# A transform-and-expert kernel: second product three rounds behind the first, a new calendar, working buffers 32 bytes later

## The chip, the cores and the metric

One core of a Trainium2 chip runs the program. The metric is device time in microseconds (us), the median of several executions; a lower time is better. The kernel before takes 2706.86 us (three runs, 2706.52 to 2708.56).

## What is computed

Two stages follow each other on 8 sequences of 3008 tokens of 256 numbers each, in float32. Cut to what matters:

```python
X  = rfft(x, axis=1)                       # along the 3008 tokens
Yr = X.real @ w_r - X.imag @ w_i + b_r
Yi = X.real @ w_i + X.imag @ w_r + b_i
Y  = soft_threshold(Yr, 0.01) + 1j * soft_threshold(Yi, 0.01)
y  = irfft(Y, n=3008, axis=1)              # 24064 tokens of 256
h  = maximum(y @ w_in, 0)                  # 256 -> 2048
out = (h * h) @ w_out                      # 2048 -> 256
```

## The kernel before

Products are made in float32 accuracy from a high and a low part of each operand (float32r): a high part is a copy on ACT, the low part a subtraction on DVE, and `mm3` (L182 to L184) issues three matmuls for one product.

**Start.** `start()` transforms the first two sequences partly, loads and splits the weights, and makes the first chunk of transformed tokens. It ends 144.9 us into the span. The change touches it only in the addresses of its buffers.

**Main loop.** The tokens are cut in 47 chunks of 512 columns, the 2048 hidden features in 8 groups; 47 x 8 = 376 rounds. A round r of the main loop (L904 to L932) does, in this order of issue:

- `mm1` (PE, L182 to L184): the first product of round r, 12 matmuls of 512 columns into the PSUM tile `ph`, of which there is one (two banks).
- `squares` (ACT, L863 and L864): two Relu from `ph` into `g`, then a square in place. As soon as the Relu are done, `ph` is free for the next `mm1`.
- places "p1" (PE) and "e" (ACT): pieces of the transform that stand in the calendar for this round.
- the high part `gh` of the round before (ACT, L916).
- `mm2` (PE, L878 and L882): the second product, `LAG` = 2 rounds behind, 21 matmuls of 256 columns into the four banks of `po`, 14 with `gh` and 7 with `gl`. Over the 8 rounds of a chunk it adds up in these banks.
- `sums` (DVE, L869 to L871) on `g`, and the low part `gl` of the round before (DVE, L927).
- place "p2" (PE), then, in the last round of a chunk, `put_together` (ACT L889, DVE L890 to L896): it reads the four banks of `po`, and the output is stored. The next chunk's first `mm2`, one round later, writes the same banks.
- places "a" (ACT) and "v" (DVE).

**Transform pieces.** For the sequences 2 to 7 there are pieces of three kinds. An A piece (`plan_a`, `psa`, 6 matmuls of 256 columns) is evacuated by ACT (L679). A pair (`plan_b`) has `psb` (8 matmul records, evacuated by ACT, L223), two rounds on the mix `psm1`, `psm2` (18 matmuls of 256 columns, evacuated by DVE, L233 and L234), and later `psc` (3 matmuls of 512 columns, evacuated by ACT, L754). A D piece (`plan_d`, `psd`, 8 records) is evacuated by ACT (L784) and by the two `unfold` instructions of DVE (L275, L276). All of them share two PSUM banks, `ps_f`, in turn; the mix takes both. The other six banks are `ph` and `po`.

**Calendar.** `pair_rounds` fixes the rounds of the pairs; `spread` places the A and D pieces by a planner's cost, which adds up the work of the engines in each round and keeps A and D pieces out of the rounds of a mix. All pieces but the mix stand at "p1", between `mm1` and `mm2`, and up to three of them in one round. What is given to the places "a" and "v" is issued last in its round: the unfold of a D piece stands behind `gl` on DVE.

Of the kernel before, what the change touches and what calls it, by code (L numbers as in the profile page):

```python
# [9 lines left out]
F32 = mybir.dt.float32  # L10
F32R = mybir.dt.float32r
# [4 lines left out]
P = 128  # L16
# [4 lines left out]
NPAIR = NR // 2  # L21
# [117 lines left out]

def pair_rounds(nb):  # L140

    out = {1: [1, 3, 5, 7, 9, 11, 13, 15, 17, 19, 22, 25]}
    for b in range(2, nb):
        last = 25 + 48 * (b - 1)
        out[b] = [last - (3 if b == 2 else 4) * (NPAIR - 1 - i) for i in range(NPAIR)]
    return out


# [1 line left out]
def fft_mix_moe(ctx: ExitStack, tc: tile.TileContext, xp, xu, w_r, w_i, b_r, b_i,  # L150
# [75 lines left out]
    def sum_x(x):  # L226
        nc.vector.tensor_add(x[:, 2], x[:, 0], x[:, 1])
# [380 lines left out]
    kept = []  # L608
    start()

    sb = ctx.enter_context(tc.tile_pool(name="sb", bufs=1))
    ps_f = ctx.enter_context(tc.tile_pool(name="ps_f", bufs=2, space=bass.MemoryType.PSUM))
    ps_h = ctx.enter_context(tc.tile_pool(name="ps_h", bufs=1, space=bass.MemoryType.PSUM))
# [8 lines left out]
    def opnd(name, dt, bufs):  # L622
        return tl(name, (P, NPR, HALF), dt, bufs=bufs)

    rounds = pair_rounds(B)
    last = nch * NU
    plan = {}
    works = np.zeros((last + 64, 3))

    def at(r, place, do):  # L630
        plan.setdefault((r, place), []).append(do)
# [5 lines left out]
    def note(r, *steps):  # L637
        for d, *w in steps:
            works[r + d] += w

    PAIR_WORK = ((0, .9, .6, .4), (1, 0, .8, 1.), (2, 2.1, 0, 1.4), (3, 0, 0, 1.1), (4, 0, 1.8, 0),
                 (5, 0, .6, .7), (7, .7, .6, 0))
    A_WORK = ((-3, 0, 0, .8), (-2, 0, .6, .7), (0, .7, .6, 0))
    D_WORK = ((0, .9, .4, .8), (1, 0, .7, .7))
    SUM_WORK = (0, 0, .3, 2.9)

    def plan_a(b, i, r):
        g, w = GROUPS[i]
        n, tab = NR * w, 0 if w == W else 2
        s = {}  # L650

        def load():
            if i == 0:
                scratch1(b)
            s["t"] = tl("ld", bufs=2, name="xin")[:n]
            load_x(b, i, s["t"])

        def folded():
            s["f"] = tl("f", name="f")[:n]
            fold(s["f"], s["t"])  # L660

        def high():
            s["h"] = tl("fh", dt=F32R)[:n]
            nc.scalar.copy(s["h"], s["f"])

        def low():
            s["l"] = tl("fl", dt=F32R)[:n]
            nc.vector.tensor_sub(s["l"], s["f"], s["h"].bitcast(F32))

        def points():  # L670
            s["o"] = pst("psa")[:n]
# [12 lines left out]
        at(r - 2, "a", high)  # L684
        at(r - 2, "v", low)
        at(r, "p1", points)
        at(r, "e", out)

    def plan_b(b, i, r):
        s = {}  # L690
# [66 lines left out]
        at(r - 1, "load", load)  # L757
        at(r, "p1", points)
        at(r, "e", take)
        at(r, "v", lambda: sum_x(s["x"]))  # L760
        at(r + 1, "a", high)
        at(r + 1, "v", low)
        at(r + 2, "p2", mix)
        at(r + 2, "v", biased)
        at(r + 3, "v", threshold)
        at(r + 4, "a", turned)
        at(r + 5, "a", zhigh)
        at(r + 5, "v", zlow)
        at(r + 7, "p1", back)
        at(r + 7, "e", out)  # L770

    def plan_d(i, r, later):
        s = {}

        def load():
            s["t"] = tl("din")
            load_d(i, s["t"])

        def points():
            s["ps"] = points_d(i, s["t"], pst("psd"))  # L780

        def take():
            s["v"] = const.tile([P, 2 * NR * W], F32, tag="dv", name="dv").rearrange("p (k m) -> p k m", k=2)
            nc.scalar.copy(s["v"][:, :, :s["ps"].shape[3]], s["ps"][:, :, 1])  # L784

        def unfolded():
            s["x"] = const.tile([P, 2 * N1 * W], F32, tag="dx", name="dx").rearrange("p (k m) -> p k m", k=2)
            unfold(i, s["ps"], s["v"], s["x"])

        at(r - 1, "load", load)  # L790
        at(r, "p1", points)
        at(r, "e", take)
        at(r, "v", unfolded)
        for n, piece in enumerate(pieces(i)):
            q = later if n else r + 1
            at(q, "a", lambda piece=piece: high_x(piece, s["x"]))
            at(q, "v", lambda piece=piece: low_x(piece, s["x"]))

    for b, rs in rounds.items():
        for r in rs:  # L800
            note(r, *PAIR_WORK)
    for c in range(nch):
        works[c * NU + NU + 1] += SUM_WORK[1:]

    mixes = {r + 2 for rs in rounds.values() for r in rs}
    def spread(n, lo, hi, work, apart):

        best = [{} for _ in range(n)]
        for i in range(n):
            for r in range(lo, hi + 1):  # L810
                if r in mixes:
                    continue
                cost = sum(max(0., float(np.sum(works[r + d] + w))) ** 2 - float(np.sum(works[r + d])) ** 2
                           for d, *w in work)
                before = min(((c, q) for q, (c, _) in best[i - 1].items() if q <= r - apart),
                             default=None) if i else (0., ())
                if before is not None:
                    best[i][r] = before[0] + cost, (best[i - 1][before[1]][1] if i else ()) + (r,)
        got = min(best[-1].values())[1]
        for r in got:  # L820
            note(r, *work)
        return got

    begin = 3
    for b in range(2, B):
        end = rounds[b][0] - 3
        got = spread(len(GROUPS), begin, end, A_WORK, 2)
        begin = max(got[-1] + 2, rounds[b][0] - 12)
        for i, r in enumerate(got):
            plan_a(b, i, r)  # L830
# [6 lines left out]
    free = 2  # L837
    for c in range(1, nch):
        own = [i for i in range(len(flat)) if begins[i] // CH == c]
        parts = [[i for i in own if flat[i][0] == b] for b in sorted({flat[i][0] for i in own})]  # L840
        for n, part in enumerate(parts):
            b = flat[part[0]][0]
            lo = max(NU * (c - 1), free, rounds[b][-1] + 9 if b else 2)
            got = spread(len(part), lo, NU * c - 3 - sum(map(len, parts[n + 1:])), D_WORK, 1)
            free = got[-1] + 1
            for i, r in zip(part, got):
                plan_d(i, r, NU * c)

    def mm1(c, j):
        ph = ps_h.tile([P, 2, CH], F32, tag="h", name="ph")  # L850
# [48 lines left out]
                              in_=o[k].rearrange("p t m -> p (t m)"))  # L899

    hid, split_, pos = {}, {}, {}
    LAG = 2
    with tc.manual_schedule():
        for r in range(last + LAG):  # L904
            c, j = divmod(r, NU)
            run(r, "load")
            if r < last:
                ph = mm1(c, j)
                g = squares(ph)
                hid[r] = g  # L910
            run(r, "p1")
            run(r, "e")
            k = r - 1
            if k in hid:
                split_[k] = opnd("gh", F32R, 2), opnd("gl", F32R, 2)
                nc.scalar.copy(split_[k][0], hid[k])  # L916
            k = r - LAG
            if k >= 0:
                cc, jj = divmod(k, NU)
                if jj == 0:  # L920
                    pos[cc] = [ps_o.tile([P, 512], F32, tag=f"o{i}", name=f"po{i}") for i in range(4)]
                mm2(jj, pos[cc], *split_.pop(k))
            if r < last:
                sums(g)
            if r - 1 in hid:
                gh, gl = split_[r - 1]
                nc.vector.tensor_sub(gl, hid.pop(r - 1), gh.bitcast(F32))  # L927
            run(r, "p2")
            if k >= 0 and jj == NU - 1:
                put_together(cc, pos.pop(cc))  # L930
            run(r, "a")
            run(r, "v")  # L932
    assert not plan, sorted(plan)
# [38 lines left out]
```

## Time and profile before

| what | value |
|---|---|
| median of three runs | 2706.86 us |
| profiled execution, its own time | 2706.33 us |
| its span | 2704.2 us |
| PE busy | 2580.7 us (95%) |
| PE weight loads busy | 2288.4 us (85%) |
| DVE busy | 2112.6 us (78%) |
| ACT busy | 1982.9 us (73%) |
| chain that ended last | PE 72%, ACT 11%, DVE 7%, issue 7% |

The span is what the trace covers; 2.1 us of the profiled execution lie around it. PE is the engine with the most work. A matmul's record lasts longer than the time after which the next one starts, so the busy time of PE covers a part of the time in which it waits.

### The profile page before, as it was taken

Reading aid. Unit: us, or ns where it says so; the run is one execution under the profiler, and the core shown is the slowest. Engines: PE = TensorE matmul, PEld = TensorE weight load, DVE = VectorE, ACT = ScalarE, POOL = GpSimd, SP = SyncE. Lnnn points to the kernel's source line nnn. Section 1 sums busy time; section 2 is a strip of 40 time slices with the busy share of each in tenths; the row PEclk is TensorE's granted clock in tenths of the full one; section 3 lists DMA queues with packets and bytes.
Section 4 is the critical chain, followed back from the end, with each engine's and each line's share of the span. In section 5 each row is a group of like instructions: output and inputs, shape, how many; then the busy total and the mean of one; then the engine's idle time right before and its main releaser. Section 6 shows DMA issues by size and latency. Waiting matters only on the chain.

```text
span 2704.2 us, 41768 instructions
## 1 busy us (share of the span) xinstructions
PE 2580.7 (95%) x16496; PEld 2288.4 (85%) x16496; DVE 2112.6 (78%) x3155; ACT 1982.9 (73%) x2764; POOL 48.2 (2%) x57
## 2 busy tenths in 40 slices
PE   7889999999999999999999999999999999999998
PEld 4578888888888889888888888888888998888887
DVE  5777887877788878877888788887887778777776
ACT  4667776767777777777787777877777777776766
POOL 1500000000000000000000000000000000000000
PEclk8999999999999999999999999999999999999999
DMA  8522222211112111121112111211111111001000
GB/s 261 182 67 65 65 65 69 65 50 60 56 57 69 57 57 56 60 65 46 56 60 68 54 57 53 75 53 51 57 56 48 38 39 51 31 24 35 16 27 16
DMA packets 113092, 164.57 MB, mean 61 GB/s; under 512 B 9584, under 2 KB 63074, under 8 KB 112706
## 3 DMA queue, kind: packets, MB, share of 16 engines
q1 hardware_dynamic: 112898, 161.91, 19.3%
q8 instruction: 131, 2.15, 0.3%
q14 instruction: 63, 0.52, 0.1%
HBM read 86.90 MB, written 74.97 MB: 60 GB/s over the span
## 4 chain that ended last, share of the span: by engine, by line
PE 72%; ACT 11%; DVE 7%; issue 7%; DMA 1%; SPq 0%; DVEq 0%; ACTq 0%
PE po L878 17%; PE ph L184 10%; PE ph L182 10%; PE ph L183 10%; PE po L882 9%; ACT gh L916 4%; ACT g L863 4%; PE psd L268 3%; PE psm L184 2%; PE psm L182 2%; PE psm L183 2%; PE psb L219 1%; DVE gl L927 1%; PE psc L182 1%; ACT x L223 1%
## 5 line engine op out<-in xcount | busy, mean ns | idle before, releaser
L927 DVE TENSOR_TENSOR gl<-g,gh 128x1792 fp32r<-128x1792 f32 x376 | 761.2, 2025 | 144.2 <-ACT gh L916 144.1
L863 ACT ACTIVATE g<-ph 128x512 f32<-128x512 f32 x752 | 408.4, 595 | 592.0 <-PE ph L184 590.9
L878 PE MATMUL po<-gh,wo 128*128 128x256 f32 x5264 | 703.6, 284 | 29.2 <-DVE o L891 17.9
L878 PEld LDWEIGHTS po<-gh,wo 128*128 128x128 f32 x5264 | 657.9, 189 | 57.5 <-DVE o L895 16.7
L916 ACT CAST gh<-g 128x1792 fp32r<-128x1792 f32 x376 | 636.2, 1692 | 0.2 <-DVE g L871 0.2
L182 PE MATMUL ph<-xt,wi 128*128 128x512 f32 x1504 | 592.7, 394 | 10.1 <-DVE dx L276 8.8
L184 PE MATMUL ph<-xt,wi 128*128 128x512 f32 x1504 | 591.1, 393 | 0.0
L183 PE MATMUL ph<-xt,wi 128*128 128x512 f32 x1504 | 590.7, 393 | 0.0
L869 DVE TENSOR_TENSOR g<-g 128x512 f32<-128x512 f32 x376 | 259.9, 691 | 332.7 <-ACT g L864 331.6
L864 ACT ACTIVATE g<-g 128x1024 f32<-128x1024 f32 x376 | 398.9, 1061 | 11.9
L882 PE MATMUL po<-gl,wo 128*128 128x256 f32 x2632 | 369.1, 280 | 0.2 <-DVE gl L927 0.2
L184 PEld LDWEIGHTS ph<-xt,wi 128*128 128x128 f32 x1504 | 283.3, 188 | 64.6
L882 PEld LDWEIGHTS po<-gl,wo 128*128 128x128 f32 x2632 | 334.9, 188 | 0.4 <-DVE gl L927 0.4
L182 PEld LDWEIGHTS ph<-xt,wi 128*128 128x128 f32 x1504 | 283.5, 188 | 59.0 <-ACT xt L280 9.0
L183 PEld LDWEIGHTS ph<-xt,wi 128*128 128x128 f32 x1504 | 283.2, 188 | 47.9
L871 DVE TENSOR_TENSOR g<-g 128x256 f32<-128x256 f32 x376 | 159.9, 425 | 12.9
L870 DVE TENSOR_TENSOR g<-g 128x256 f32<-128x256 f32 x376 | 160.0, 425 | 12.8
L184 PE MATMUL psm<-wm,xl 128*128 128x256 f32 (+1 forms) x552 | 162.3, 294 | 0.7 <-DVE xl L712 0.6
L182 PE MATMUL psm<-wm,xh 128*128 128x256 f32 (+1 forms) x552 | 162.1, 294 | 0.3 <-ACT x L223 0.3
L183 PE MATMUL psm<-wm,xh 128*128 128x256 f32 (+1 forms) x552 | 159.9, 290 | 0.0
L268 PEld LDWEIGHTS psd<-tD,din 120*128 120x128 f32 (+1 forms) x832 | 105.7, 195 | 50.5 <-ACT g L863 30.5
L268 PE MATMUL psd<-tD,din 120*128 120x120 f32 (+1 forms) x832 | 117.2, 285 | 32.2 <-ACT g L863 25.5
(102 smaller groups left out, 2572.4 us busy)
## 6 DMA issues: line engine op xcount, KB each, us to landing
bin<-s SPq DMA_DIRECT2D x96, 256.0 KB
s<-evc SPq DMA_DIRECT2D x96, 256.0 KB
outT_dram<-o SPq DMA_DIRECT2D x94, 256.0 KB
din<-s SPq DMA_DIRECT2D x96, 240.0 KB
xin<-in_xp_dram SPq DMA_DIRECT2D x72, 240.0 KB
s<-eva SPq DMA_DIRECT2D x72, 240.0 KB
s<-eva SPq DMA_DIRECT2D x22, 192.0 KB
w<-in_moe_w_in_dram SPq DMA_DIRECT2D x8, 512.0 KB
```

What stands on the lines that cost most here:

```text
L182: nc.tensor.matmul(out, l0, r0, start=start, stop=False, **kw)
L183: nc.tensor.matmul(out, l0, r1, start=False, stop=False, **kw)
L184: nc.tensor.matmul(out, l1, r0, start=False, stop=stop, **kw)
L268: nc.tensor.matmul(ps[:, k, part], t[:n, s:s + P], tD[:n, tab + part, :n], start=True, stop=True)
L863: nc.scalar.activation(g[:, 2 * a:2 * a + 2], ph[:, a].rearrange("p (t m) -> p t m", t=2), AF.Relu)
L864: nc.scalar.activation(g[:, 0:4], g[:, 0:4], AF.Square)
L869: nc.vector.tensor_sub(g[:, 4:6], g[:, 1:4:2], g[:, 0:2])
L870: nc.vector.tensor_sub(g[:, 6], g[:, 3], g[:, 4])
L878: nc.tensor.matmul(out, wo_[k][j][:, s], gh[:, s], start=j == 0 and half == 0 and k == 0, stop=False, skip_group_check=True)
L882: nc.tensor.matmul(out, wo_[0][j][:, s], gl[:, s], start=False, stop=j == NU - 1, skip_group_check=True)
L916: nc.scalar.copy(split_[k][0], hid[k])
L927: nc.vector.tensor_sub(gl, hid.pop(r - 1), gh.bitcast(F32))
```

## The change

The second product runs three rounds behind the first (`LAG` 3). `gh` and `gl` keep two buffers each. A round has new places: "p1" and "p2" are both open to transform pieces (before and behind `mm2`), with "e" (ACT) and, behind `sums`, "e2" as the places of evacuation of the first, and "f" (ACT) and "f2" (DVE), behind the split of `g`, as those of the second. `put_together` of a chunk's last round comes before the split of `g` on both engines. The mix's DVE work goes from "v" to "f2", a pair's high part of `x` from the next round to "f" of its own, its `psc` from "p1", seven rounds on, to "p2", five or six rounds on. The planner keeps one piece per place, may set an A piece (with a price, a D piece) beside a mix, and counts ACT and DVE alone. A tile `gap` of 32 bytes in the constant pool moves every working buffer behind it: in the built program they began at byte 138,240 of each partition (a multiple of 256) and now at 138,272.

```diff
-    out = {1: [1, 3, 5, 7, 9, 11, 13, 15, 17, 19, 22, 25]}
+    out = {1: [1 + 2 * i for i in range(NPAIR)]}
     for b in range(2, nb):
-        last = 25 + 48 * (b - 1)
-        out[b] = [last - (3 if b == 2 else 4) * (NPAIR - 1 - i) for i in range(NPAIR)]
+        last = 23 + 48 * (b - 1)
+        out[b] = [last - (2 if b == 2 else 3) * (NPAIR - 1 - i) for i in range(NPAIR)]
...
+    const.tile([P, 8], F32, name="gap", tag="gap")
     sb = ctx.enter_context(tc.tile_pool(name="sb", bufs=1))
...
+    LAG = 3
...
+    BACK = {b: 5 + (b > 2) for b in range(1, B)}
+    EVAC = {"p1": ("e", "e2"), "p2": ("f", "f2")}
...
-        at(r, "v", lambda: sum_x(s["x"]))
-        at(r + 1, "a", high)
-        at(r + 1, "v", low)
+        at(r, "e2", lambda: sum_x(s["x"]))
+        at(r, "f", high)
+        at(r, "v", low)
         at(r + 2, "p2", mix)
-        at(r + 2, "v", biased)
-        at(r + 3, "v", threshold)
-        at(r + 4, "a", turned)
-        at(r + 5, "a", zhigh)
-        at(r + 5, "v", zlow)
-        at(r + 7, "p1", back)
-        at(r + 7, "e", out)
+        at(r + 2, "f2", biased)
+        at(r + 2, "v", threshold)
+        at(r + 3, "a", turned)
+        at(r + 4, "a", zhigh)
+        at(r + 4, "v", zlow)
+        at(r + BACK[b], "p2", back)
+        at(r + BACK[b], "f", out)
...
-        at(r, "p1", points)
-        at(r, "e", take)
-        at(r, "v", unfolded)
+        at(r, p, points)
+        at(r, act, take)
+        at(r, dve, unfolded)
...
+            if not ends:
+                high()
             if k >= 0:
                 if jj == 0:
                     pos[cc] = [ps_o.tile([P, 512], F32, tag=f"o{i}", name=f"po{i}") for i in range(4)]
                 mm2(jj, pos[cc], *split_.pop(k))
+            run(r, "p2")
             if r < last:
-                sums(g)
-            if r - 1 in hid:
-                gh, gl = split_[r - 1]
-                nc.vector.tensor_sub(gl, hid.pop(r - 1), gh.bitcast(F32))
-            run(r, "p2")
-            if k >= 0 and jj == NU - 1:
+                sums(hid[r])
+            run(r, "e2")
+            if ends:
                 put_together(cc, pos.pop(cc))
+                high()
+            else:
+                low()
+            run(r, "f")
+            run(r, "f2")
+            if ends:
+                low()
             run(r, "a")
             run(r, "v")
```

The first place is DVE in a round at the end of a chunk that has no transform piece (g: hidden values, gl: their low part, po: banks of the second product, o: output). Before:

```order
L869 TENSOR_TENSOR g<-g 128x512
L870 TENSOR_TENSOR g<-g 128x256
L871 TENSOR_TENSOR g<-g 128x256
L927 TENSOR_TENSOR gl<-g,gh 128x1792
L890 TENSOR_TENSOR o_26249<-po_25889,o_26249 128x256
L891 TENSOR_TENSOR o_26249<-po_25888,o_26249 128x256
L892 TENSOR_TENSOR o_26250<-po_25889,o_26249 128x256
L893 TENSOR_TENSOR o_26249<-po_25890,o_26249 128x256
L894 TENSOR_TENSOR o_26250<-po_25890,o_26250 128x256
L895 TENSOR_TENSOR o_26249<-po_25890,o_26249 128x256
L896 TENSOR_TENSOR o_26250<-o_26250,po_25891 128x256
```

and now:

```order
L883 TENSOR_TENSOR g<-g 128x512
L884 TENSOR_TENSOR g<-g 128x256
L885 TENSOR_TENSOR g<-g 128x256
L904 TENSOR_TENSOR o_26270<-po_25931,o_26270 128x256
L905 TENSOR_TENSOR o_26270<-po_25930,o_26270 128x256
L906 TENSOR_TENSOR o_26271<-po_25931,o_26270 128x256
L907 TENSOR_TENSOR o_26270<-po_25932,o_26270 128x256
L908 TENSOR_TENSOR o_26271<-po_25932,o_26271 128x256
L909 TENSOR_TENSOR o_26270<-po_25932,o_26270 128x256
L910 TENSOR_TENSOR o_26271<-o_26271,po_25933 128x256
L937 TENSOR_TENSOR gl<-g,gh 128x1792
```

The seven instructions on `po` stood behind `gl`, and now stand ahead of it.

The second place is DVE in a round with a D piece, between two chunk ends (psd: the D piece's PSUM bank, dv and dx: its halves, xt: the tokens' parts for the first product, x: a pair's values). Before:

```order
L869 TENSOR_TENSOR g<-g 128x512
L870 TENSOR_TENSOR g<-g 128x256
L871 TENSOR_TENSOR g<-g 128x256
L927 TENSOR_TENSOR gl<-g,gh 128x1792
L227 TENSOR_TENSOR x<-x 128x256
L285 TENSOR_TENSOR xt_13914<-dx,xt_13913 128x2x235
L275 TENSOR_TENSOR dx<-psd,dv 128x2x120
L276 TENSOR_TENSOR dx<-psd,dv 128x2x115
```

and now, in another round of the same kind (zl: low part of a pair's turned values):

```order
L883 TENSOR_TENSOR g<-g 128x512
L884 TENSOR_TENSOR g<-g 128x256
L885 TENSOR_TENSOR g<-g 128x256
L275 TENSOR_TENSOR dx<-psd,dv 128x2x120
L276 TENSOR_TENSOR dx<-psd,dv 128x2x115
L937 TENSOR_TENSOR gl<-g,gh 128x1792
L749 TENSOR_TENSOR zl<-z,zh 128x512
L285 TENSOR_TENSOR xt_7482<-dx,xt_7481 128x2x170
```

The two instructions that read `psd` stood last in their round, and now stand right behind the three of `sums`.

The third place is ACT in a round that has a pair's `psb` (x, xh: the pair's values and their high part; z: turned values; evc: what `psc` left; fh: high part of an A piece). Before:

```order
L863 ACTIVATE g<-ph 128x512 x2
L864 ACTIVATE g<-g 128x1024
L223 COPY x<-psb 128x2x2x128
L784 COPY dv<-psd 128x240
L916 CAST gh<-g 128x1792
L736 COPY z<-e 64x256
L737 ACTIVATE z<-e,sg 64x256
L736 COPY z<-e 64x256
L737 ACTIVATE z<-e,sg 64x256
L280 CAST xt_13913<-dx 128x2x235
```

and now:

```order
L877 ACTIVATE g<-ph 128x512 x2
L878 ACTIVATE g<-g 128x1024
L223 COPY x<-psb 128x2x2x128
L932 CAST gh<-g 128x1792
L758 COPY evc<-psc 128x512
L712 CAST xh<-x 128x768
L740 COPY z<-e 64x256
L741 ACTIVATE z<-e,sg 64x256
L740 COPY z<-e 64x256
L741 ACTIVATE z<-e,sg 64x256
L668 CAST fh<-f 120x512
```

The D piece's copy has gone to other rounds, and the evacuation of an earlier pair's `psc` and the high part of `x` now stand between the split of `g` and the turning. In the order's waits the copy into `gh` now waits for the matmuls of the same round's `mm2`, which read the same buffer's old content.

Counted in the order, the main loop's pieces stand as follows.

| what stands in a round | before | now |
|---|---|---|
| two or three pieces ahead of `mm2` | 93 | 0 |
| `psb` and `psd` (both ahead; now one on either side) | 28 | 6 |
| `psa` or `psb` ahead and the mix behind | 9 | 52 |
| `psd` ahead and the mix behind | 0 | 4 |
| `psb` ahead and `psc` behind | 0 | 50 |
| no piece | 54 | 88 |

## Rows read from the trace of the kernel before

**Rows 1.** Busy time by stage; columns: stretch, length, engines' busy time, PEclk, DMA share, GB/s

```profile
0.00:144.90 144.90, 107.99 (x377) 63.70 (x377) 90.41 (x148) 70.21 (x134) 46.11 (x56) 0.88 0.72 215
144.90:2698.10 2553.20, 2472.56 (x16120) 2224.73 (x16120) 2019.62 (x3001) 1912.68 (x2631) 2.11 (x1) 1.00 0.17 52
...
740.00:1500.00 760.00, 740.57 (x4858) 665.67 (x4857) 614.87 (x928) 578.69 (x811) 0.00 (x0) 1.00 0.19 59
```

**Rows 2.** PE's groups by line from 144.9 us on; busy, mean ns, idle before

```profile
L878 PE MATMUL po<-gh,wo 128*128 128x256 f32 x5264 | 703.6, 284 | 29.2 <-DVE o L891 17.9 <-DVE o L895 8.1 <-ACT gh L916 1.4
L182 PE MATMUL ph<-xt,wi 128*128 128x512 f32 x1504 | 592.7, 394 | 10.1 <-DVE dx L276 8.8 <-ACT g L863 1.3
L882 PE MATMUL po<-gl,wo 128*128 128x256 f32 x2632 | 369.1, 280 | 0.2 <-DVE gl L927 0.2
L182 PE MATMUL psm<-wm,xh 128*128 128x256 f32 x504 | 141.9, 282 | 0.3 <-ACT x L223 0.3
L268 PE MATMUL psd<-tD,din 120*128 120x120 f32 (+1 forms) x808 | 113.7, 285 | 29.7 <-ACT g L863 25.5 <-ACT eva L679 2.3 <-DMA din<-s 1.2
L219 PE MATMUL psb<-tB,bin 128*128 128x128 f32 x672 | 91.0, 279 | 4.6 <-DVE e L233 3.4 <-ACT g L863 1.0 <-DVE xt L285 0.3
L182 PE MATMUL psa<-fh,tAs 120*120 120x256 f32 (+1 forms) x156 | 45.4, 291 | 12.6 <-DVE e L233 12.6
L182 PE MATMUL psc<-zh,tMs 128*128 128x512 f32 x84 | 39.1, 466 | 2.1 <-DVE e L233 1.9
```

**Rows 3.** Timeline of PE: a chunk's end, then a round with nothing else

```profile
2657.48 0.39 PE L182 MATMUL ph<-xt,wi 128*128 128x512 f32 x1
...
2661.98 1.18 PE L878 MATMUL po<-gh,wo 128*128 128x256 f32 x8 [1.57 <-DVE o L891]
2663.41 0.97 PE L878 MATMUL po<-gh,wo 128*128 128x256 f32 x6 [0.25 <-DVE o L895]
2664.22 0.98 PE L882 MATMUL po<-gl,wo 128*128 128x256 f32 x7
2665.04 0.40 PE L182 MATMUL ph<-xt,wi 128*128 128x512 f32 x1
...
2667.80 1.80 PE L878 MATMUL po<-gh,wo 128*128 128x256 f32 x14
...
2670.26 0.40 PE L182 MATMUL ph<-xt,wi 128*128 128x512 f32 x1
```

**Rows 4.** Timeline of DVE at the same chunk's end

```profile
2659.01 2.02 DVE L927 TENSOR_TENSOR gl<-g,gh 128x1792 fp32r<-128x1792 f32 x1
2660.96 0.42 DVE L890 TENSOR_TENSOR o<-po,o 128x256 f32<-128x256 f32 x1
...
2662.94 0.42 DVE L895 TENSOR_TENSOR o<-po,o 128x256 f32<-128x256 f32 x1
```

**Rows 5.** Timeline of a round with `psb` and `psd`

```profile
1437.84 1.06 PE L219 MATMUL psb<-tB,bin 128*128 128x128 f32 x8
...
1439.48 0.39 DVE L276 TENSOR_TENSOR dx<-psd,dv 128x230 f32<-128x230 f32 x1
1439.97 1.12 PE L268 MATMUL psd<-tD,din 120*128 120x120 f32 x8 [1.07 <-ACT g L863]
```

**Rows 6.** Timeline of ACT in a round with an A piece

```profile
1416.70 1.09 ACT L863 ACTIVATE g<-ph 128x512 f32<-128x512 f32 x2
...
1417.82 1.06 ACT L864 ACTIVATE g<-g 128x1024 f32<-128x1024 f32 x1
...
1418.78 0.57 ACT L679 COPY eva<-psa 120x512 f32<-120x512 f32 x1
```

**Rows 7.** Timeline of the last rounds

```profile
2692.69 1.91 PE L878 MATMUL po<-gh,wo 128*128 128x256 f32 x14 [1.39 <-ACT gh L916]
```

**Rows 8.** Timeline of PE in a `psc`

```profile
1431.16 0.39 PE L183 MATMUL psc<-zl,tMs 128*128 128x512 f32 x1
1431.40 0.40 PE L184 MATMUL psc<-zh,tMs 128*128 128x512 f32 x1
```

More of the change, by code (lines that the diff above doesn't have):

```diff
@@ L627, in fft_mix_moe @@
     plan = {}
-    works = np.zeros((last + 64, 3))
+    works = np.zeros((last + 64, 2))
     def at(r, place, do):
@@ L639, in note, with plan_a @@
             works[r + d] += w
[L641 to L647, printed above, removed]
+    PAIR_WORK = ((0, .6, .4), (1, .8, 1.), (2, 0, 2.5), (3, 1.8, 0), (4, .6, .7), (6, .6, 0))
+    BACK = {b: 5 + (b > 2) for b in range(1, B)}
+    A_WORK = ((-3, 0, .8), (-2, .6, .7), (0, .6, 0))
+    D_WORK = ((0, 1., 1.5),)
+    SUM_WORK = ((1, .3, 2.9),)
+    EVAC = {"p1": ("e", "e2"), "p2": ("f", "f2")}
+    def plan_a(b, i, r, p):
         g, w = GROUPS[i]
@@ L685, in plan_a @@
         at(r - 2, "v", low)
-        at(r, "p1", points)
-        at(r, "e", out)
+        at(r, p, points)
+        at(r, EVAC[p][0], out)
     def plan_b(b, i, r):
@@ L759, in plan_b, with plan_d @@
         at(r, "e", take)
-        at(r, "v", lambda: sum_x(s["x"]))
-        at(r + 1, "a", high)
-        at(r + 1, "v", low)
+        at(r, "e2", lambda: sum_x(s["x"]))
+        at(r, "f", high)
+        at(r, "v", low)
         at(r + 2, "p2", mix)
-        at(r + 2, "v", biased)
-        at(r + 3, "v", threshold)
-        at(r + 4, "a", turned)
-        at(r + 5, "a", zhigh)
-        at(r + 5, "v", zlow)
-        at(r + 7, "p1", back)
-        at(r + 7, "e", out)
-    def plan_d(i, r, later):
+        at(r + 2, "f2", biased)
[5 more added lines that the diff above has]
+        at(r + BACK[b], "f", out)
+    def plan_d(i, r, p, later):
         s = {}
@@ L788, in unfolded @@
             unfold(i, s["ps"], s["v"], s["x"])
+        act, dve = EVAC[p]
         at(r - 1, "load", load)
-        at(r, "p1", points)
-        at(r, "e", take)
-        at(r, "v", unfolded)
+        at(r, p, points)
+        at(r, act, take)
+        at(r, dve, unfolded)
         for n, piece in enumerate(pieces(i)):
-            q = later if n else r + 1
-            at(q, "a", lambda piece=piece: high_x(piece, s["x"]))
-            at(q, "v", lambda piece=piece: low_x(piece, s["x"]))
+            q, act, dve = (later, "e", "e2") if n else (r, "a", "v") if p == "p1" else (r + 1, "e", "e2")
+            at(q, act, lambda piece=piece: high_x(piece, s["x"]))
+            at(q, dve, lambda piece=piece: low_x(piece, s["x"]))
+    taken = set()
+    mixes = set()
     for b, rs in rounds.items():
@@ L801, in fft_mix_moe, with spread, plan_all_a @@
             note(r, *PAIR_WORK)
+            mixes.add(r + 2)
+            use = {(r, 0), (r + 2, 1), (r + BACK[b], 1)}
+            assert not use & taken
+            taken |= use
     for c in range(nch):
-        works[c * NU + NU + 1] += SUM_WORK[1:]
-    mixes = {r + 2 for rs in rounds.values() for r in rs}
-    def spread(n, lo, hi, work, apart):
+        note(c * NU + NU + LAG - 2, *SUM_WORK)
+    def spread(n, lo, hi, work, apart, beside):
+        slots = [(r, h) for r in range(lo, hi + 1) for h in range(2)
+                 if (r, h) not in taken]
         best = [{} for _ in range(n)]
         for i in range(n):
[L810 to L815, printed above, removed]
+            for r, h in slots:
+                cost = .3 * h + .3 * ((r, 1 - h) in taken) + beside * (r in mixes) + sum(
+                    float(np.sum((works[r + d] + w) ** 2 - works[r + d] ** 2)) for d, *w in work)
+                before = min(((c, q) for q, (c, _) in best[i - 1].items() if q[0] <= r - apart),
                              default=None) if i else (0., ())
                 if before is not None:
-                    best[i][r] = before[0] + cost, (best[i - 1][before[1]][1] if i else ()) + (r,)
+                    best[i][r, h] = before[0] + cost, (best[i - 1][before[1]][1] if i else ()) + ((r, h),)
         got = min(best[-1].values())[1]
-        for r in got:
+        taken.update(got)
+        for r, _ in got:
             note(r, *work)
[L822 to L830, printed above, removed]
+        return [(r, f"p{h + 1}") for r, h in got]
+    def plan_all_a(b, begin):
+        got = spread(len(GROUPS), begin, rounds[b][0] - 3, A_WORK, 2, 0)
+        for i, rp in enumerate(got):
+            plan_a(b, i, *rp)
+        return max(got[-1][0] + 2, rounds[b][0] - 12)
     for b, rs in rounds.items():
@@ L836, in fft_mix_moe @@
         at(0, "v", lambda i=i, xf=xf: low_x(pieces(i)[1], xf))
-    free = 2
+    free, begin, b = 2, 3, 2
     for c in range(1, nch):
+        while b < B and rounds[b][0] <= NU * c:
+            begin = plan_all_a(b, begin)
+            b += 1
         own = [i for i in range(len(flat)) if begins[i] // CH == c]
@@ L841, in fft_mix_moe @@
         for n, part in enumerate(parts):
[L842 to L847, printed above, removed]
+            at_b = flat[part[0]][0]
+            lo = max(NU * (c - 1), free, rounds[at_b][-1] + BACK[at_b] + 3 if at_b else 2)
+            got = spread(len(part), lo, NU * c - 3 - sum(map(len, parts[n + 1:])), D_WORK, 1, 20)
+            free = got[-1][0] + 1
+            for i, rp in zip(part, got):
+                plan_d(i, *rp, NU * c)
     def mm1(c, j):
@@ L901, in fft_mix_moe @@
     hid, split_, pos = {}, {}, {}
-    LAG = 2
     with tc.manual_schedule():
@@ L908, in fft_mix_moe, with high, low @@
                 ph = mm1(c, j)
-                g = squares(ph)
-                hid[r] = g
+                hid[r] = squares(ph)
             run(r, "p1")
             run(r, "e")
[L913 to L916, printed above, removed]
             k = r - LAG
+            cc, jj = divmod(k, NU)
+            ends = k >= 0 and jj == NU - 1
+            def high():
+                if r - 1 in hid:
+                    split_[r - 1] = opnd("gh", F32R, 2), opnd("gl", F32R, 2)
+                    nc.scalar.copy(split_[r - 1][0], hid[r - 1])
+            def low():
+                if r - 1 in hid:
+                    gh, gl = split_[r - 1]
+                    nc.vector.tensor_sub(gl, hid.pop(r - 1), gh.bitcast(F32))
+            if not ends:
+                high()
             if k >= 0:
-                cc, jj = divmod(k, NU)
                 if jj == 0:
```

## The prediction

> **What bounds the kernel now.** I read the busy time by stage first, then PE's groups by line, then single rounds on the timeline. After a start of 144.9 us a main stretch of 2553.2 us follows, in which PE is busy for 2472.6 us, ACT for 1912.7 and DVE for 2019.6, with PE's granted clock at 1.00, the upper of its two levels [rows 1]. So PE is the bound, and the question is how much of the stretch is matmuls at their pace and how much is waiting.
>
> The pace comes from a round with nothing but its two products: its first matmul starts at 2665.04, `mm2` at 2667.80 and the next round at 2670.26 [rows 3]. That is 2.76 us for 12 matmuls of 512 columns, 0.230 each, and 2.46 us for 21 of 256 columns, 0.117 each; 5.22 us in all. A `psc` matmul of 512 columns takes 0.24 to the next one (1431.16 to 1431.40) [rows 8], and the 8 records of a `psb`, busy for 1.06 us with the last of them 0.28 long, follow each other after 0.111 us ((1.06 - 0.28) / 7) [rows 2, 5]. I take that for `psd` too.
>
> The counts are in PE's groups, where L182 stands for one of three lines of equal count [rows 2]. First product 3 x 1504 x 0.230 = 1038 us; second product (5264 + 2632) x 0.117 = 925; mix and A pieces 3 x (504 + 156) x 0.117 = 232; `psc` 3 x 84 x 0.235 = 59; `psd` and `psb` (808 + 672) x 0.111 = 164. Together 2418 us. The stretch has 2553.2, so **about 135 us are gaps** (134 in the count by rounds below). The idle time of PE in it is only 2553.2 - 2472.6 = 81 us, because a record (0.39 us) outlasts the pace (0.23) and so covers the first 0.2 us of each gap.
>
> Where the gaps lie I read from the starts of all 376 rounds, each round's length less its own matmuls at the pace. Four kinds:
>
> A. The 46 rounds that begin a new chunk in `po`, 62 us. In the bare one shown the round goes from 2657.48 to 2665.04, 7.56 us for 5.22: a gap of 2.34. PE waits 1.57 for L891, the last reader of the first bank, and 0.25 for L895, the last of the third [rows 3]. These stand on DVE behind `gl`, which took 2.02 us from 2659.01 [rows 4]. A piece at "p1" covers its own length of the gap, so that most of the 46 show 0.3 to 1.5 us.
>
> B. 27 other rounds with both `psb` and `psd` ahead of `mm2`, 34 us, most of them 1.3 each. `psb` ends its pace at 1437.84 + 0.89 = 1438.73, but `psd` starts at 1439.97, 0.1 us after L276 has read the bank's old content (1439.48 + 0.39) [rows 5]. That instruction is the unfold of the round before, last in DVE's queue. The releaser named there, ACT's `g`, had long been done.
>
> C. The rest of the rounds, 36 us, of which 25 in the first 85, where the calendar is densest; the first five rounds have 4.
>
> D. The end, 2 us: the last `mm2` but one waits 1.39 for `gh` [rows 7], and a little for `gl`.
>
> **The change part by part.** No matmul, no ACT and no DVE instruction is added or dropped, so the 2418 us stay, and only gaps move.
>
> *put_together ahead of `gl`.* It can then start when `sums` ends, at 2659.01 instead of 2660.96 in the same round, 1.95 us earlier; its ACT copy needs only `mm2`'s end. L891 would end at 2661.83 - 1.95 = 2659.9, before `mm1`'s pace ends at 2660.24: no wait. L895 would end at 2661.4 and PE gets to its bank after 8 matmuls, at 2660.24 + 0.94 = 2661.2: 0.2 to 0.3 us are left [rows 3, 4]. Any piece in either of the two rounds (0.7 us or more) covers this; by the order seven chunk ends have none. So A goes from 62 to **3 us** (bounds 0 and 46 x 0.3 = 14). What is late next is `gl`, by 2.9 us, but it is read two rounds on instead of one.
>
> *One piece per place, unfold right behind `sums`.* A `psd` bank is free about 2 us (the length of `gl`) sooner, and two pieces of a round no longer follow each other directly. B goes from 34 to 0, but four rounds have `psd` ahead of a mix, which needs both banks: unfold ends some 4.5 us after the Relu began (Relu and square 2.2, `sums` 1.6, two unfolds 0.75), PE reaches `psm2` after 0.9 + 2.5 + 0.7 = 4.1. With ACT a little late I take 0.75 each, **3 us**.
>
> *A new wait: A piece or `psb` ahead, mix behind, 52 rounds.* `psm2` must wait for ACT's copy of the first piece. ACT's Relu starts at 1416.70 and the copy ends at 1418.78 + 0.57 = 1419.35, 2.65 us later [rows 6]. PE needs 0.7 for the piece, 2.46 for `mm2` and 6 x 0.117 for `psm1`, 3.9 us, so there is 1.2 us of room. Queued behind this are the rest of the mix and the next `mm1`. I take 0 as long as ACT is not late by more than the room. Bounds: 0, and 52 x 0.8 = 42 us if ACT is 2 us late in all of them.
>
> *Does ACT come late?* In the dense stage it is busy for 578.7 of 760 us [rows 1], 76%, and 80% once the gaps are gone. The order puts eleven instructions in a round that has `psb` and `psc`, about 8 us of work where PE has 0.9 + 2.46 + 0.7 + 2.76 = 6.8, then seven, then four in the round of the mix. It is late by about 1 us once in three rounds and has caught up before the mix. The new wait of `gh` for the same round's `mm2` (L932, with the pieces at "f" and "a" queued behind it) costs nothing: the 14 matmuls that read the old `gh` end 1.64 us into `mm2`, while ACT comes there only 2.1 us after `mm1` [rows 6].
>
> *`LAG` 3 at both ends.* Rounds 1 and 2 have no `mm2`: PE has 3.6 us a round (2.76 and a piece), DVE some 5.3 (1.6 + 2.0 and two pieces), so up to 2 x 1.7 us are added to the 4 of the first five rounds; I take **8 us** in all. At the end the last `gh` has one more `mm2` (2.46 us) to be ready behind, so the 2 us of D go to **0**.
>
> *The rest of C* (32 us) came from three pieces in a round and from unfolds at a round's end; the new order has neither. I keep **8 us** for loads and lateness I can't see (bounds 0 and 32).
>
> *32 bytes.* No row compares addresses directly. In the built program the first product reads operands that lie 32 bytes past a multiple of 64, `psc` reads operands on a multiple, and both run at 0.23 to 0.24 us per 512 columns [rows 3, 8]. I take **0**; each ns on the second product's pace would be 7.9 us. The Trainium skill (DMA: Bandwidth & Descriptors, How a descriptor splits into AXI transactions) speaks against the shift: a descriptor that doesn't start on 256 bytes begins with a transaction at the boundary below. For 2 KB rows that would be one beat more in 64, by my estimate under 2 us in the start, where DMA is busy for 0.72 of the time, and nothing behind it; no run here shows it.
>
> *Sum:* 3 + 3 + 0 + 8 + 0 + 8 = 22 us of gaps instead of 134. 2706.3 (the profiled execution's own time, 2.1 above its span and 0.5 below the median) - 112 = **2594 us**.
>
> **The rivals.** *The gaps come back on ACT and DVE* (late evacuation). Each of the 84 pairs would cost 0.8 us in its mix or in the next `psb`, which waits for L233: 84 x 0.8 = 67, that is 2661; 2635 with half of it. For it: all evacuations are now due within one round. Against: 1.2 us of room and 20% of ACT free.
>
> *Slower, by the address.* If the second product, whose moving operand alone changes from a multiple of 64 to 32 past it, ran at 0.133 instead of 0.117, its 7896 matmuls would lose 7896 x 0.016 = 126 us: 2720. It decides from 14.2 ns on (112 us over 7896 matmuls). Against it speaks that 512 columns cost the same at either address.
>
> *Faster pace by the address.* At 0.113 it would gain 32 us: 2562. The Trainium skill (TensorE: Matmul & The Clock Gate, Back-to-back issue gap) gives N / 2.4 + 2.5 ns, 109 and 216 ns, where the trace has 117 and 230; by that the second product has 63 us to gain, 2531. Nothing in the rows says that addresses cause the difference.
>
> *The change doesn't do what it says* (something else paces the rounds): about 2706. Against it, bare rounds run without any gap [rows 3].
>
> **How the numbers follow.** Forecast, 2575 to 2620: 0.75. Gaps come back, 2620 to 2665: 0.12. Slower: 0.05. Faster pace: 0.05. No effect: 0.03. The likeliest is 2594. Leaving out what is above 2640 and below 2568 leaves about 0.8 to 0.85 inside. Faster by over 0.2% (about 5 us, what a measurement of this kernel can tell from no change) has the first, the second and the fourth, 0.92; within 0.2% 0.03; slower 0.05.
>
> **What would show it.** In the profile after: PE's wait for the `po` readers (L891, L895 of before) nearly gone; no `psd` waiting 1 us behind `psb`; 5.22 us in bare rounds as before; `psm2` waits for `eva` or `x` copies small. It would be wrong if the pace of either product moved by some ns, if `psm` or `psb` collected waits of 0.5 us and more per pair, or if loads (`bin`, `din`) came late because SP's queue, which stores in order, waits for the later evacuations at "f".

## The result, and the profile after

The changed kernel takes 2603.08 us (median of four runs, 2598.85 to 2604.28), the kernel before 2707.22 on the same chip. The ratio is 0.961 with a 95% interval of 0.960 to 0.963. The forecast was 2594; 9 us of the expected gain did not come.

First the page of the profile after: busy us, share of the span and instructions of each engine, and the chain that ended last.

```profile
span 2602.5 us, 41936 instructions
...
PE 2540.2 (98%) x16496; PEld 2284.6 (88%) x16496; DVE 2107.2 (81%) x3155; ACT 1993.8 (77%) x2764; POOL 47.9 (2%) x57
...
PE 82%; DVE 6%; ACT 5%; issue 1%; DMA 1%; DVEq 0%; SPq 0%; ACTq 0%
```

The engines do the same work in a shorter time. The busy time by stage (columns as in [rows 1]; the first row is the main stretch of after, the next two are short windows that are spoken of at the end):

```profile
146.30:2596.30 2450.00, 2431.58 (x16120) 2220.04 (x16120) 2013.78 (x3001) 1923.22 (x2631) 2.11 (x1) 1.00 0.17 54
1673.00:1675.00 2.00, 0.77 (x7) 0.81 (x8) 0.33 (x1) 1.97 (x4) 0.00 (x0) 1.00 0.47 143
1675.00:1678.50 3.50, 3.50 (x22) 3.50 (x21) 3.06 (x8) 1.00 (x3) 0.00 (x0) 0.61 0.37 107
```

The main stretch went from 2553.2 to 2450.0 us, 103.2 less; the start took 1.4 more, the 6 us behind the last matmuls the same. With matmuls at the pace of before (2418 us) there are 32 us of gaps where there were 135, against 22 forecast.

PE's waits in this stretch (us in total, times, longest us; the wait for `dx` is that of the very first `mm1`, at the end of the start):

```profile
PE ph L182 <- DVE dx L276: 8.7, 1, 8.7
PE psb L219 <- DVE e L233: 5.7, 10, 0.9
PE psd L268 <- DMA din<-s: 5.1, 6, 1.8
PE psm L182 <- DVE dx L276: 3.2, 4, 0.9
PE ph L182 <- ACT g L877: 2.4, 2, 1.3
PE po L892 <- DVE o L909: 0.8, 3, 0.3
PE psm L182 <- ACT x L223: 0.6, 1, 0.6
PE po L892 <- DVE o L905: 0.2, 1, 0.2
```

The waits for the readers of `po` (L891 and L895 of before, L905 and L909 now) fell from 17.9 and 8.1 us [rows 2] to 0.2 and 0.8. The 26 waits of a `psd` behind a `psb` are gone. Two kinds are new at this size: `psb` waiting for L233, and `psd` waiting for its load.

A chunk's end after, on DVE and PE, in a round with an A piece ahead of `mm2` (timeline; columns as in [rows 3, 4]):

```profile
1344.54 0.43 DVE L885 TENSOR_TENSOR g<-g 128x256 f32<-128x256 f32 x1
...
1344.88 0.42 DVE L904 TENSOR_TENSOR o<-po,o 128x256 f32<-128x256 f32 x1
...
1345.34 0.42 DVE L905 TENSOR_TENSOR o<-po,o 128x256 f32<-128x256 f32 x1
...
1346.87 0.41 DVE L909 TENSOR_TENSOR o<-po,o 128x256 f32<-128x256 f32 x1
1346.89 1.82 PE L892 MATMUL po<-gh,wo 128*128 128x256 f32 x14
...
1347.52 2.02 DVE L937 TENSOR_TENSOR gl<-g,gh 128x1792 fp32r<-128x1792 f32 x1
...
1348.55 0.98 PE L896 MATMUL po<-gl,wo 128*128 128x256 f32 x7
```

The readers of `po` follow `sums` directly and are done before the 14 matmuls need their banks, where in [rows 3, 4] L927 of 2.02 us stood between. `gl` now ends at 1349.5, after this round's matmuls on `gl` have begun (1348.55): with `LAG` 3 these don't read it.

Where I speak of gaps below, each round's length less its own matmuls at the pace of before is meant, summed over a kind of rounds. Matmuls that ran slower while the granted clock was low count into the gaps too (last section). A round that begins a chunk is r mod 8 = 2 at `LAG` 2 and 3 at `LAG` 3.

| kernel | time, us | all gaps | rounds that begin a chunk | r mod 8 = 5 (`psb` and `psd` in before) |
|---|---|---|---|---|
| before | 2707 | 132 | 62 | 36 |
| after | 2603 | 31 | 7 | 2 |

### The profile page after: what moved, and what is told of

The parts are those of the page before. It is cut to its first block, busy times and chain, and to the rows that moved or that the text cites. A ratio compares the mean times of both kernels' runs of the same rounds, so it can differ in the third digit from the quotient of the medians.

```text
span 2602.5 us, 41936 instructions
## 1 busy us (share of the span) xinstructions
PE 2540.2 (98%) x16496; PEld 2284.6 (88%) x16496; DVE 2107.2 (81%) x3155; ACT 1993.8 (77%) x2764; POOL 47.9 (2%) x57
## 4 chain that ended last, share of the span: by engine, by line
PE 82%; DVE 6%; ACT 5%; issue 1%; DMA 1%; DVEq 0%; SPq 0%; ACTq 0%
PE po L892 21%; PE ph L182 12%; PE ph L184 12%; PE ph L183 12%; PE po L896 11%; PE psd L268 3%; PE psb L219 3%; PE psm L182 2%; PE psm L183 2%; PE psm L184 2%; DVE gl L937 2%; ACT g L877 1%; DMA din<-s 1%; ACT g L878 1%; DVE g L883 1%
## 5 line engine op out<-in xcount | busy, mean ns | idle before, releaser
L932 ACT CAST gh<-g 128x1792 fp32r<-128x1792 f32 x376 | 638.4, 1698 | 19.9 <-PE po L892 16.6
L219 PEld LDWEIGHTS psb<-tB,bin 128*128 128x128 f32 x768 | 100.6, 194 | 36.0 <-issue 17.8
```

The lines of the kernel that those rows point to most:

```text
L219: nc.tensor.matmul(ps[:, k, :, q, :], tv[:, q, k], tB[:, 0:r + 2:r + 1], start=True, stop=True)
L932: nc.scalar.copy(split_[r - 1][0], hid[r - 1])
```

## The experiments

**The address, alone and left out.** In the kernel before, the tile is added; in the one after, it is dropped:

```diff
+    const.tile([P, 8], F32, name="gap", tag="gap")
```

> The kernel before with the 32-byte tile alone. Gaps theory: no gap goes, the pace alone can move: mix 117.9 to 114.6 ns, second product 117.0 to 117.8 ns, 2700 to 2712. Address theory: a good part of the 104 us, 2680 or less.

> The changed kernel without the 32-byte tile: working buffers begin at byte 138,240 again. If the gain is gaps that went by order alone, only the pace of matmuls moves: the mix back from 114.6 to 117.9 ns (1512 x 3.3 = 5 us more), the second product back from 117.8 to 117.0 ns (7896 x 0.8 = 6 us less), the first product back from 229.3 to 230.3 (4512 x 1.0 = 5 us more): 2600 to 2610. If the shift carries a part of the gain that the order doesn't explain, 2620 or more.

Measured: before with the tile 2703.94 us, ratio 0.999 (0.9981 to 0.9998), 2.5 us less by the medians; after without it 2603.67, ratio 0.962 (0.961 to 0.963), against 2603.08 with it. So the 32 bytes are worth at most some 5 us in the old order and nothing that the times can tell in the new one, and nearly the whole gain of 104 us is the new order's. (What they do below the sum stands in the last section.)

**`put_together` moved back or forward.** In after, it goes behind `gl` again, and behind the places "f" and "f2"; in before, with `LAG` 2, ahead of `gl`. The diff of the second:

```diff
             if r < last:
                 sums(g)
+            if k >= 0 and jj == NU - 1:
+                put_together(cc, pos.pop(cc))
             if r - 1 in hid:
...
-            if k >= 0 and jj == NU - 1:
-                put_together(cc, pos.pop(cc))
```

> The changed kernel with put_together behind the split of g again, on both engines. Gaps theory: the next chunk's first second product waits for its banks again, 1 to 1.3 us in each of 46 rounds, 2650 to 2665, and the rows show the wait for the last readers of the banks. Rival, that three rounds of distance already took that wait away: 2600 to 2610.

> The kernel before (second product two rounds behind) with put_together ahead of gl at chunk ends. Gaps theory: the bank wait goes, but gl is ready 2.7 us later and is read one round on: in a bare round gl ends at 2663.8 where its matmuls are due at 2662.2, a wait of 1.6 us in place of 2.34. So only some 0.6 us x 46 = 28 us are won: about 2680, and the rows show PE waiting for gl. Rival, that order alone is enough: 2650.

Measured: 2663.39 (0.984, 0.983 to 0.986), 60 us lost, as expected; the gaps of chunk begins went from 7 to 74 us (some 12 of them are matmuls at the lower clock, see the last section). The other direction, 2702.34 (0.998, 0.997 to 0.999), gave 5 us and not 27. Its waits name the reason (PE, main stretch):

```profile
PE po L882 <- DVE gl L929: 30.3, 33, 1.3
PE psd L268 <- ACT g L863: 25.3, 26, 1.3
```

The waits for L891 and L895 are gone, and 33 waits for the low part stand in their place: at `LAG` 2 the round behind a chunk's end reads the `gl` that has just been moved back.

**`LAG` 3 left out of after.** The same calendar, `LAG` 2.

> The changed kernel with LAG 2 in place of 3 and the same calendar. Theory: put_together ahead of gl needs the third round, since at LAG 2 the round that begins a chunk reads the gl that now ends some 3 us later; 27 such rounds have no piece ahead of mm2 and cost some 2.0 us each, 19 have one and cost 1.1: 76 us on top of 2603, 2650 to 2690. Rival, the two places of a round and put_together's place alone do it and LAG 3 is only for safety: 2600 to 2615.

Measured: 2631.28 us (0.972, 0.970 to 0.973), 28 more than after. The mechanism is the expected one:

```profile
PE po L896 <- DVE gl L937: 30.0, 30, 1.3
```

The size is not: a bare chunk begin lost 1.4 us, not 2.0, one with an A piece 0.55, and rounds with r mod 8 = 4 won 14 us back (17 to 4). Why they did wasn't separated: with `LAG` 2 a chunk also ends one round earlier, farther from these rounds. `LAG` 3 is worth 28 us in this calendar.

**`LAG` 3 alone, and with `put_together` ahead of `gl`, in the kernel before.**

```diff
-    LAG = 2
+    LAG = 3
```

> The kernel before with the second product three rounds behind, nothing else. Gaps theory: the bank wait stands behind gl as before, so the 62 us stay; 2 us go at the end and up to 3 come at the start: 2700 to 2710. Rival, that the distance itself is the gain: 2610 to 2650.

> The kernel before with three rounds of distance and put_together ahead of gl. Gaps theory: the late gl is now hidden, 62 us fall to about 3: 2645 to 2652. If the distance and the order each give their part alone, it is the sum of the two runs beside it.

Measured: 2780.75 (1.027, 1.025 to 1.029) and 2789.02 (1.030, 1.029 to 1.032). Both expectations missed, the second by 140 us; as the sum of the two single edits it would have been some 2776. The timeline of `LAG` 3 alone shows the two causes. A chunk's begin:

```profile
1241.75 0.42 DVE L891 TENSOR_TENSOR o<-po,o 128x256 f32<-128x256 f32 x1
...
1242.32 1.17 PE L878 MATMUL po<-gh,wo 128*128 128x256 f32 x8 [1.15 <-ACT g L863]
...
1243.68 0.97 PE L878 MATMUL po<-gh,wo 128*128 128x256 f32 x6 [0.19 <-DVE o L895]
...
1244.68 1.70 ACT L916 CAST gh<-g 128x1792 fp32r<-128x1792 f32 x1 [1.30 <-PE po L878]
```

At `LAG` 3 a chunk begins one round later. There, in 33 of the 46 rounds, the old calendar has no piece at "p1" but a mix at "p2", which covers nothing: PE waits for L891 (it ended 0.15 us before; the releaser named, ACT's `g`, is nothing that `mm2` touches) for its full length. Gaps of chunk begins went from 62 to 101 us. With `put_together` ahead of `gl` they stayed at 104: the mix of that round reads a low part (`xl`, L712) that stands at the end of DVE's row, behind both, and 36 waits for it (58.9 us) stand where the wait for L891 was.

The last row shows the second cause: ACT's cast into `gh` waits for the matmuls of the same round's `mm2`, which still read that buffer (128 such waits, 130 us in all). A round with two pieces ahead of `mm2`, further on:

```profile
1254.46 1.69 ACT L916 CAST gh<-g 128x1792 fp32r<-128x1792 f32 x1 [0.92 <-PE po L878]
...
1256.18 2.02 DVE L927 TENSOR_TENSOR gl<-g,gh 128x1792 fp32r<-128x1792 f32 x1 [1.73 <-ACT gh L916]
...
1260.11 0.39 DVE L276 TENSOR_TENSOR dx<-psd,dv 128x230 f32<-128x230 f32 x1
...
1260.60 1.12 PE L268 MATMUL psd<-tD,din 120*128 120x120 f32 x8 [1.70 <-ACT g L864]
```

Late `mm2`, late `gh`, late `gl`, late unfold (L276), and the next `psd` waits longer, which makes its own `mm2` late. Each of the 22 rounds with `psb` and `psd` at r mod 8 = 5 now loses 1.9 us instead of 1.25; the gaps of that phase went from 36 to 58 us. In all the gaps grew by 75 us, the loss. A third buffer for `gh`, which would take this wait away, wasn't tried.

**`LAG` 3 with the old calendar one round later**, to tell the two causes apart, without and with `put_together` ahead of `gl`.

```diff
-    out = {1: [1, 3, 5, 7, 9, 11, 13, 15, 17, 19, 22, 25]}
+    out = {1: [2, 4, 6, 8, 10, 12, 14, 16, 18, 20, 23, 26]}
...
-        last = 25 + 48 * (b - 1)
+        last = 26 + 48 * (b - 1)
...
-            got = spread(len(part), lo, NU * c - 3 - sum(map(len, parts[n + 1:])), D_WORK, 1)
+            got = spread(len(part), lo, NU * c - 2 - sum(map(len, parts[n + 1:])), D_WORK, 1)
...
-    LAG = 2
+    LAG = 3
```

> The kernel before with LAG 3 alone, but its calendar one round later (each pair, its SUM_WORK and the D pieces' last round), so that the rounds that begin a new chunk in po have an A or D piece ahead of mm2 again, where with LAG 3 and the old calendar 33 of them had a bare mm2 and a mix. Theory: of the 74 us that LAG 3 alone cost, some 38 are this (rounds that begin a chunk: 62 us of gaps before, 101 with LAG 3 alone) and go; some 30 come from the cast of gh, which with LAG 3 waits for the same round's mm2 and makes gl, the unfold behind it and the next psd late where two pieces stand ahead of mm2 (1.9 us a psb and psd round against 1.25), and stay. So 2720 to 2750, 2736 taken. Rival one, the place in the calendar is all of it: 2700 to 2712. Rival two, the wait of gh is all of it: 2770 to 2785.

> The same (LAG 3, calendar one round later) with put_together ahead of gl. Theory: gl is now read two rounds on, so what LAG 2 gave back to the wait for gl is really gained, and the 62 us of the rounds that begin a chunk fall to 10 or 20: 40 to 50 us below the kernel with LAG 3 and the later calendar, that is 2675 to 2705. Rival, put_together's place is worth as little as with LAG 2 (5 us): 2720 to 2745.

Measured: 2932.06 (1.083, 1.081 to 1.084) and 2895.05 (1.069, 1.067 to 1.071). As times both missed everything, and by a flaw of the edit: a chunk's last D piece, one round later, comes too late for the chunk's own first product.

```profile
PE ph L182 <- ACT xt L280: 79.0, 27, 3.5
PE ph L183 <- DVE xt L285: 47.3, 27, 3.1
```

The rounds on either side of a new chunk's first product (r mod 8 = 7 and 0) hold 209 us of gaps, where the kernel before has 13; PE's granted clock over the span is 0.961 instead of 0.990. The two waits shown are 126 us; much of what is left should be matmuls at the lower clock, by an estimate from the two clocks 87 us (0.039 x 2926.5 - 0.010 x 2704.2). The other rounds can still be read one by one:

| kernel | chunk begins | rounds with `psb` and `psd` |
|---|---|---|
| before | 62 | 36 |
| `LAG` 3 | 101 | 58 |
| `LAG` 3, calendar one later | 60 | 58 |
| the same, `put_together` ahead of `gl` | 27 | 55 |

The first cause goes with the calendar and the second stays, each with the size that it had; and `put_together` ahead of `gl` is worth 34 us at chunk begins here where it was worth 4 at `LAG` 2. This rests on rounds of a disturbed kernel; a clean one, with time left for the D pieces, wasn't run.

**The unfold's place and the two places of a round.** In after, the unfold goes last in its round again ("v" in place of "e2" and "f2"); in before, with all pieces at "p1", it goes right behind `sums`. In both, the split of the D piece's values into high and low parts moves along with it, in after to the next round, in before into the same one. From the diff of the second:

```diff
-        at(r, "v", unfolded)
+        at(r, "e2", unfolded)
```

> The changed kernel with the unfold of a D piece last in its round again (place v). If the early unfold is what removed the 34 us of psd behind psb, they come back: about 2637. If two places per round did it (the bank's next user now comes a whole second product later), only the four rounds with psd ahead of a mix lose 2 us more each, and some mixes a little: 2610 to 2620.

> The kernel before with the unfold of a D piece right behind sums and its split at the end of the same round. Gaps theory: psd no longer waits 1.3 us behind psb in 27 rounds, 34 us less: about 2673. Rival, that the wait is for ACT's g, as the row names it: no change, 2700 to 2708.

Measured: 2614.25 (0.966, 0.965 to 0.967), 11 lost: four mixes with a `psd` ahead now wait 13 us in all, up to 3.6 each; and 2677.96 (0.989, 0.988 to 0.991), 29 won, with the gaps at r mod 8 = 5 down from 36 to 4. Both were as expected. So either edit removes the wait of `psd`: with two places the unfold may come late, with an early unfold the pieces may stand side by side.

**A version that mends what is left.** In after, the mix's `biased` at "f2" comes ahead of `gl` in every round, and a D piece at "p1" doesn't follow one at "p2" of the round before:

```diff
             if ends:
                 put_together(cc, pos.pop(cc))
                 high()
-            else:
-                low()
             run(r, "f")
             run(r, "f2")
-            if ends:
-                low()
+            low()
...
             free = got[-1][0] + 1
+            if got[-1][1] == "p2":
+                taken.add((free, 0))
```

> The changed kernel with two small edits: the mix's biased at f2 stands ahead of gl in every round, not at chunk ends alone, and a D piece at p1 never follows one at p2 of the round before (two of the five moved pieces waited for their load with the one din buffer). Theory: the psb that waits for L233 (50 rounds with psb and psc, 9 us in all, 8.4 of it in ten rounds) waits no more, and the late loads of rounds 180 and 228 (5 us) are gone: 2603 less 8 to 14, 2589 to 2596. Rival, something else comes due at the same point (ACT's copy, or the load one round later): 2598 to 2606.

Measured: 2590.99 us (2590.60 to 2593.45; 0.957, 0.956 to 0.958), 12 us under the changed kernel and the fastest of all. First a round of after behind a chunk's end, then the same round here:

```profile
1892.69 2.02 DVE L937 TENSOR_TENSOR gl<-g,gh 128x1792 fp32r<-128x1792 f32 x1
...
1894.62 0.68 DVE L233 TENSOR_TENSOR e<-psm,bias 128x512 f32<-128x512 f32 x1
1895.36 1.16 PE L219 MATMUL psb<-tB,bin 128*128 128x128 f32 x8 [0.88 <-DVE e L233]
```

```profile
1881.48 0.68 DVE L233 TENSOR_TENSOR e<-psm,bias 128x512 f32<-128x512 f32 x1
...
1882.88 2.02 DVE L940 TENSOR_TENSOR gl<-g,gh 128x1792 fp32r<-128x1792 f32 x1
...
1883.11 1.05 PE L219 MATMUL psb<-tB,bin 128*128 128x128 f32 x8
```

The wait of `psb` is gone (its 50 rounds: 9.2 us of gaps to 1.0), the late loads fell in part (8.6 to 5.1; the two rounds with a `psd` at "p2" just before are without gaps, the others wait a little longer), and all gaps from 31 to 18 us. The expectation held.

## Why the prediction was right, and where it was short

- **Pace** (2418 us kept): held. The gaps by rounds, 31 us, and those by the length of the stretch, 32, agree.
- **A, 62 to 3:** right in mechanism, though some 7 of the 62 were matmuls at the lower clock and not waits (last section). A bare chunk begin keeps 0.33 us, as worked out; together, without those of other entries here, they have 5.3. The first experiments show that it needs both halves: `put_together`'s place without `LAG` 3 gives 5 us, and `LAG` 3 with `put_together` last loses 60.
- **B, 34 to 3:** right. The four rounds with `psd` ahead of a mix lose 1.03 us each, not 0.75: 4.1.
- **The new wait, 0:** right. The 43 rounds with an A piece or `psb` ahead of a mix (the first five rounds aside) have no gap (they are 2.5 us under the pace of before, for a reason in the last section). Of all mixes one, in round 3, waits for ACT's copy (0.6 us in the list of waits above); later ACT was never late by the 1.2 us of room.
- **`gh`'s wait, 0:** right for this order, but the working was short. It set 1.64 us against 2.1 with no piece ahead of `mm2`; the cast did wait 26 times, 24 of them behind a piece, 16.6 us in all, without a wait of PE for `gh`. The kernel with `LAG` 3 and the old calendar shows what it costs with two pieces.
- **`LAG` 3 at the ends, 8 and 0:** 6.2 and 0.
- **The rest, 8:** this is the term that was mis-sized; no row gave it. It measured 17.6: 9.2 in the 50 rounds with `psb` and `psc`, where `psb` waits for L233, and 8.6 in rounds with a `psd`, most of it behind late loads. What took it down from 32 wasn't tested by itself. The rival "the gaps come back on ACT and DVE" had the right place, "the next `psb`, which waits for L233", and about the right price, 0.8 us, but ten pairs pay it and not 84. (Half of its 67 us makes 2628, not the 2635 given there.) All ten stand two rounds behind the last of a chunk, where `put_together` has held DVE up. In five of them an unfold falls into that last round; they lose 1.05 to 1.15 us each, and nothing when the unfold goes last. The other five lose 0.5 to 0.6, wherever the unfold stands. A load that comes late was named among the things that would go wrong, with SP's queue as the cause. In two rounds, 5.1 of the 8.6 us, the cause is another, the one `din` buffer, when `psd` stands at "p2" of one round and "p1" of the next. In the others it is SP's queue, not behind an evacuation at "f" but behind the stores of the chunk that has just ended, which wait for `put_together`. Here the `psd` before had ended 35 us earlier, so the buffer was free:

```profile
708.13 0.85 SPq L912 DMA_DIRECT2D outT_dram<-o  x2
709.07 2.06 SPq L259 DMA_DIRECT2D din<-s  x1
...
713.82 0.35 PE L268 MATMUL psd<-tD,din 96*128 96x96 f32 x1 [0.70 <-DMA din<-s]
```

- **32 bytes, 0:** right in the sum within some us, but a sum of opposite terms; the second product's pace, the rivals' ground, moved by 0.4 to 1.0 ns. The Trainium skill's rule on a descriptor that doesn't start on 256 bytes (DMA: Bandwidth & Descriptors, How a descriptor splits into AXI transactions) would have shown in the start. The first `mm1` came at 145.0 to 148.5 us in the six kernels with the tile, and at 142.4 to 146.5 in the eight without, one trace of each: the runs don't decide it.

Together: 9.6 us more in the rest, 2.3 in A, 1.1 in B and 1.4 in the start, 1.8 less in the first rounds and 2.5 less in the mixes; that is the 10 us by which the profiled execution (2604.28) missed.

## What to carry to other kernels

An edit of a pipeline's depth is not worth a sum of its own: here depth 3 cost 74 us in the old order and saved 28 in the new one, because it moved the round in which a buffer is written against the pieces that could cover the wait. Price such an edit with the calendar that it will run in, and look for the buffer that its readers now hold longer. When a tuned order has few gaps left, list for each shared bank or buffer its last reader and what stands ahead of it on that engine; the last 12 us were the places of the mix's evacuation and of a few D pieces.

## What the runs showed of the hardware

**Where the working buffers start moves the pace of matmuls, in both directions.** Mean time from one matmul to the next of the same kind, in ns, from their starts in the traces (some 4100 for the first product, 4600 for the second, 1400 for the mix, 370 for A):

| kernel | first product | second, `gh` | mix | A piece |
|---|---|---|---|---|
| before | 230.3 | 117.1 | 117.9 | 117.7 |
| before, 32 bytes later | 229.3 | 117.5 | 114.3 | 118.9 |
| after, without the 32 bytes | 230.1 | 116.9 | 118.0 | 118.1 |
| after | 229.3 | 117.8 | 114.6 | 119.0 |

For after, the second product loses some 8 us (7896 x 1.0), the mix gains 5.3 (1512 x 3.5) and the first product 3.8 (4512 x 0.85): nothing in the sum. For before the same sum is a gain of some 6 us, where 2.5 were measured (0.5 to 5). Why a kind gains or loses isn't settled. That the pace of each kind moves with the tile alone is shown in two orders, and all the kernels here fall in two groups by it: in the eight without the tile the mix stands at 117.9 to 118.4 ns and the first product at 230.1 to 230.4, in the six with it at 114.3 to 114.6 and 229.2 to 229.3. It need not be the address of a matmul's own operands: those of the first product, `wi` and `xt`, are made ahead of `gap` in the constant pool. An address chosen for each buffer wasn't tried.

**A short wait of PE can cost twice.** In after, one `psd` waits for its load:

```profile
1674.23 1.12 PE L268 MATMUL psd<-tD,din 120*128 120x120 f32 x8 [1.76 <-DMA din<-s]
...
1675.11 2.79 PE L892 MATMUL po<-gh,wo 128*128 128x256 f32 x14
...
1677.70 1.66 PE L896 MATMUL po<-gl,wo 128*128 128x256 f32 x7
```

In the 3.5 us behind it the granted clock is 0.61 (the windows above), between its two levels of 1.2 and 2.4 GHz; PE had been busy for only 0.77 of the 2.00 us before. The 14 matmuls took 2.79 us instead of 1.82, the seven 1.66 instead of 0.98, and the round lost 3.6 us for a wait of 1.8. The wait of 1.57 us in [rows 3] was not followed by it: eight matmuls there took 1.18 us.

It is not the only case. In after with `put_together` behind `gl`, seven of the chunk begins lost 3.2 to 3.9 us. Each has one wait of 1.6 to 2.1 us, and behind it a stretch at 0.50, the lower level; the other chunk begins kept the upper one. The seven stretches together are 23 us, so some 12 of the 60 us lost there are slow matmuls, by an estimate at half the pace. Two of the seven:

```profile
770.60:773.90 3.30, 3.30 (x18) 3.30 (x17) 3.23 (x8) 0.71 (x1) 0.00 (x0) 0.50 0.48 158
1098.30:1101.60 3.30, 3.21 (x15) 2.92 (x15) 2.71 (x6) 1.23 (x1) 0.00 (x0) 0.50 0.62 182
```

In the kernel before, the three chunk begins with the largest gaps (3.8, 3.8 and 6.5 us) have such stretches, 13 us in all, so by the same estimate some 7 of its 62 us are slow matmuls:

```profile
220.40:223.80 3.40, 3.40 (x16) 3.09 (x15) 1.95 (x5) 1.17 (x2) 0.00 (x0) 0.50 0.63 195
285.30:288.60 3.30, 3.30 (x13) 3.01 (x14) 2.35 (x5) 0.89 (x3) 0.00 (x0) 0.50 0.70 245
572.00:578.70 6.70, 4.92 (x23) 4.93 (x24) 3.86 (x8) 1.26 (x3) 0.00 (x0) 0.50 0.45 153
```
